# Keeping ten of twelve narrowed weight slices on chip in a recurrent attention and feed-forward kernel

## The chip, the cores and the metric

The kernel runs on one core of a Trainium2 chip. The core has a matrix engine (TensorE, PE in the profile, with its weight loads as PEld), a vector engine (VectorE, DVE), a scalar engine (ScalarE, ACT), GpSimd (POOL) and a sync engine (SyncE, SP) that does nothing here but issue transfers. Data lie in DRAM or in on-chip memory of 128 partitions; matmul results go to a small accumulator memory (PSUM). Transfers (DMA) are issued by SP, and by POOL for the attention's inputs, and are moved by 16 DMA engines. The metric is the time of one execution in device microseconds; less is better.

## The reference

Two blocks follow each other. The first is a recurrence over 768 tokens with a 40 x 40 state for each of 4 x 8 sequences; the second is a gated feed-forward layer on all 3072 tokens.

```python
for t in range(S):                     # batch 4, heads 8, S 768, head_dim 40
    y[:, :, t] = einsum('bhd,bhde->bhe', rt, state)
    Sa = einsum('bhde,bhe->bhd', state, at)
    state_decay = state * wt[:, :, None, :] - einsum('bhd,bhe->bhde', Sa, bt)
    state = state_decay + einsum('bhd,bhe->bhde', vt, kt)
x = y.transpose(0, 2, 1, 3).reshape(3072, 320)
xn = x / sqrt(mean(x * x) + 1e-06) * rms_g
g, val = xn @ w_gate, xn @ w_val       # 320 x 1536 each
out = (silu(g) * val) @ w_out          # 1536 x 320
```

The inputs of the attention are float32. The three weight matrices come as float64 and have to be narrowed to float32 by the kernel's own arithmetic.

## The kernel before

**Attention.** The tokens are cut into 24 chunks of 32, and all 32 sequences are worked on at once. `front(c)` (line 712) loads a chunk, turns it with matmuls against a unit matrix and builds, level by level (spans of 1, 2, 4, 8, 16 tokens), the products of keys and decays; its triangular matrices go through DRAM (tile `sB`) to be laid out one per partition. `inverse(c)` (line 821; the first four chunks use `early_inverse`, line 839) inverts them on VectorE in some 60 small steps with a multiply tile `tmp`, and sends them back through DRAM (`sY`). `main(c)` (line 871) does the part that depends on the chunk before: from state `ST` a right-hand side `Xs`, from it the values `VU`, the new state, a turned copy `vut` of the values, the scores, their masked levels `As`, and the read-out into `y` by level. `y` is then turned, normalised into `x`, turned again and written to the feed's input tile `xg`.

**Feed-forward.** `feed(g)` (line 1001) takes two chunks, 256 tokens, once both are there. It goes through the 12 slices of the weights in pairs, up in even groups and down in odd ones: `h64` and `h` matmuls of the gate and the value half, a Silu on ACT into `sg`, a product on VectorE into `hT`, and `out` matmuls that add into the accumulator `po`. After the last pair ACT copies `po` to tile `o`, and four transfers write it out. A slice is a tile `wf` of 128 x 960 float32 (480 KB); there are six such tiles (`WB = 6`). A narrowed slice lives in DRAM (`sW`), and a feed loads what its six tiles don't hold from the feed before: all 12 slices in the first group, 10 in the second, 6 in each of the ten others, 82 in all.

**Narrowing.** `narrow(f, part)` (line 1037) turns one half of a slice from float64 to float32. It loads the raw words into a `wf` tile that serves as staging, has ACT make the scale from the exponent in three operations into a scratch tile (`ex`, `o` or the second `xg`, in turn), has VectorE join the mantissa in three operations, and stores the half to `sW`. This is done 24 times, during the first 200 us or so.

**Order.** A recording layer (`Plan`, line 270) takes every operation as a piece with an engine and what it depends on. `plan.issue(ORDER, PAIRS)` then hands the pieces to the engines in the sequence that the text `ORDER` (line 33) gives, number by number, relative to the first piece not yet issued; `PAIRS` (line 253) names the accumulator pair that each group of matmuls takes. A dash in `ORDER` issues one filler matmul of the unit matrix into an unused part of `po` (line 1077). So each engine's sequence, SP's and POOL's queues of transfers among them, is fixed by that text; engines wait for each other by semaphores only. Buffers of a kind are handed out in turn by `Turns` (line 561). Since nearly every operation is recorded by a helper, the profile shows helper lines: 545 matmuls, 548 turns by matmul, 503 VectorE, 523, 526 and 529 ACT, 532, 535 and 538 POOL, 542 transfers.

Of the kernel before, what the change touches and what calls it, by code (L numbers as in the profile page):

```python
# [7 lines left out]
FP32 = mybir.dt.float32  # L8
# [9 lines left out]
P = 128  # L18
C = 32
LEVELS = (1, 2, 4, 8, 16)  # L20
CG = 2
WB = 6
# [11 lines left out]
- - 4 - 327 - 328 - - - 6 453 5 7 8 9 10 - 11 12 13 14 15 - 16 17 19 18 20 25 26 21 316 325 - - 313 314 324  # L34
323 - 326 318 - 315 317 93 74 83 3 94 85 73 84 82 - 320 46 43 50 61 38 - - - 60 - - 445 444 455 49 58 44 27 56
62 - 333 41 36 48 54 70 - 441 66 53 59 45 638 29 - 32 28 456 55 451 - - - 442 - 334 339 - - 337 335 338 340
349 350 23 - 342 343 354 24 353 22 355 348 351 352 - 344 - 362 336 366 364 95 - 345 367 346 - - - 347 379 360
- - - 361 363 - 359 365 - 375 75 76 376 78 - 79 - 387 77 356 357 - - 373 - 86 378 371 377 - 80 452 446 454 443
57 - 525 636 37 458 34 368 461 - 374 372 89 386 - 369 383 358 462 - 384 370 466 464 465 385 463 478 98 483 495
- 380 467 381 87 468 395 477 - - 470 471 482 - - 481 472 96 492 382 88 494 97 - 99 - 491 476 493 0 328 123 - -  # L40
102 0 - 100 320 - - 121 112 390 389 387 388 102 - - 111 123 392 471 477 487 - 478 486 - 472 98 - - 488 391 79
103 485 473 88 - - - 89 505 626 61 631 69 598 524 633 621 31 67 66 37 395 632 - - 482 - 62 623 622 28 635 625
- 33 396 624 29 397 398 399 483 400 - - 498 401 402 403 404 405 406 407 - - - - - - - 494 499 484 504 - - 394
500 511 502 496 - 104 - 408 409 410 501 411 412 413 414 - 386 - 415 - 503 416 417 418 419 420 421 422 - 641
105 646 - 106 645 643 - 642 - 107 - 423 - 424 425 - 108 497 - 510 - 644 495 426 328 99 330 329 577 427 - - 506
508 509 109 317 319 120 - 90 - 124 647 521 513 - 125 648 113 114 - 115 657 - 522 131 132 576 - 339 507 127 650
651 656 128 - 428 110 142 517 516 - 652 143 518 515 429 - 653 658 512 660 661 - 116 - 654 - 659 117 655 567
860 70 38 - 45 457 65 63 445 446 448 870 861 871 458 447 430 50 - 662 126 568 669 - 133 134 135 578 581 580
579 672 674 - 664 - - - 118 - - - 519 - 520 - - - 431 - - 432 434 433 - 435 - 436 670 437 438 569 572 570 573
571 129 663 673 675 136 137 138 525 683 - 526 527 671 684 467 528 665 529 667 679 668 682 530 531 532 687 680  # L50
686 533 534 535 536 537 538 539 540 685 541 676 677 542 514 543 544 545 546 547 548 549 550 551 552 553 554 -
119 151 140 162 160 - 163 802 141 999 152 666 582 - 574 144 678 681 583 688 147 148 689 555 1000 172 0 761 90
131 535 653 105 516 546 - - 551 - 555 - 564 - 99 659 121 657 658 660 549 550 553 554 552 654 113 650 106 - 114
109 547 655 548 115 116 117 589 590 600 118 0 406 656 590 600 508 548 554 547 825 579 657 700 701 816 509 131
101 643 115 550 551 552 118 642 119 647 702 703 116 117 124 1083 125 126 652 134 653 511 110 512 143 513 510
553 556 557 558 658 559 560 - 120 561 654 831 514 132 826 835 834 515 832 133 135 833 127 128 129 659 660 661
662 663 664 665 666 667 138 142 - 121 516 517 136 137 836 704 706 655 144 708 705 707 - 139 840 - 668 669 670
671 841 - 852 672 848 140 851 853 673 147 674 - 675 148 - 676 865 677 863 861 0 683 - 689 700 694 685 690 684
459 868 693 707 581 708 717 732 734 582 15 579 716 548 712 580 549 713 550 714 719 715 432 585 23 - - 33 21 0
- 394 11 33 32 13 0 26 25 16 861 683 - 417 418 862 681 419 851 749 750 671 571 0 708 701 569 0 569 - 5 6 416  # L60
531 572 689 532 8 533 534 9 708 535 386 704 566 14 15 16 17 - - 0 - 570 569 568 699 529 530 698 567 0 528 700
0 562 713 711 14 698 715 15 559 7 8 712 560 567 710 406 855 16 - 724 427 854 844 21 417 22 568 569 570 571 575
709 716 667 708 - 528 574 573 - 0 23 22 33 520 - 696 782 563 698 784 785 783 697 705 711 567 568 708 709 569
570 571 - 710 398 399 400 401 713 - 847 836 841 830 840 832 842 831 572 769 - - 839 - 829 521 21 0 16 - - 516
712 24 515 710 709 517 711 514 - 841 843 844 842 565 704 840 6 566 848 0 0 0 760 846 856 853 857 564 565 566
712 567 - 569 570 568 - 759 761 842 713 573 - 515 575 574 843 4 852 14 15 16 703 6 844 7 851 17 847 516 5 0
509 568 1243 703 702 846 850 858 0 9 509 858 14 15 16 860 568 569 570 753 523 21 24 23 1241 22 707 708 846 10
709 839 840 710 859 856 754 755 756 757 841 861 711 712 713 850 853 854 714 715 869 716 - 717 718 866 871 872
852 - 855 0 560 561 32 755 513 756 - 857 840 851 854 852 708 862 709 710 711 712 713 714 853 856 - 759 863 864
# [1040 lines left out]
```

## Time and profile before

| | |
|---|---|
| median of 3 runs | 1030.82 us (1029.99 to 1036.54) |
| profiled execution | 1040.74 us, span 1038.9 us |
| busy: PE, PEld | 991.8 us (95%), 813.4 us |
| busy: DVE, ACT, POOL | 834.2 us, 452.8 us, 310.1 us |
| mean granted TensorE clock | 0.970 |
| DMA | 113.03 MB in 163538 packets |
| loads of narrowed slices | 82 of 480 KB, median 4.7 us to landing |

A group row of the page names line, engine, operation, the tile written and the tiles read, the shape and the count; behind the first bar stand the group's busy time in us and the mean of one in ns, behind the second the engine's idle time just before it and what ended most of that. A row of the windows view gives a stretch, then for each engine its busy time and (x) its instructions, then the granted clock, the mean busy share of the 16 DMA engines and GB/s. A row of the waits reads: who waited, for whom, total us, times, longest. "issue" means that an engine waited for nothing that the profile shows. An engine name with a q is its sequencer, which issues transfers.

### The profile page before, as it was taken

The numbers are of one execution on the slowest core, as the hardware profiler recorded it, in microseconds if no ns is written. First come the engines' busy times: TensorE is split into PE (matmuls) and PEld (weight loads), VectorE is DVE, ScalarE is ACT, GpSimd is POOL, SyncE is SP. The second block draws the span as 40 slices with busy tenths as digits, with TensorE's granted clock in tenths as the row PEclk, the third lists the DMA queues.
The fourth block names the chain that finished last, engine by engine and source line by source line (L and its number), as shares of the span: only waits on it lengthen the run. The fifth ranks groups of instructions, "written<-read, shape, count | busy, mean of one in ns | idle before, by whom it ended". The sixth has DMA issues, their size and how long they took to land.

```text
span 1038.9 us, 56159 instructions
## 1 busy us (share of the span) xinstructions
PE 991.8 (95%) x24900; PEld 813.4 (78%) x24900; DVE 834.2 (80%) x2789; ACT 452.8 (44%) x1019; POOL 310.1 (30%) x554
## 2 busy tenths in 40 slices
PE   8968798999999999999999999999999999999998
PEld 7867686888887888888778877878777788787876
DVE  8878777887979898899888798888899789889310
ACT  5755783644452543433533443352334334341210
POOL 9624422231451224142134232242331331210000
PEclk9886898999999999999999999999999999999999
DMA  7676567465443434534433644343524533422322
GB/s 156 155 171 162 156 130 187 127 160 135 124 87 93 120 73 94 131 72 92 127 71 81 139 79 126 94 84 83 140 61 93 136 67 83 130 44 63 87 65 75
DMA packets 163538, 113.03 MB, mean 109 GB/s; under 512 B 124512, under 2 KB 142880, under 8 KB 163296
## 3 DMA queue, kind: packets, MB, share of 16 engines
q1 hardware_dynamic: 144928, 86.48, 32.9%
q0 software_dynamic: 16192, 22.64, 10.9%
q8 instruction: 195, 3.19, 1.3%
q10 hardware_dynamic: 2176, 0.33, 0.3%
q14 instruction: 47, 0.39, 0.1%
HBM read 93.39 MB, written 15.99 MB: 105 GB/s over the span
## 4 chain that ended last, share of the span: by engine, by line
PE 77%; DVE 10%; DMA 4%; issue 4%; ACT 3%; POOL 1%; SPq 1%; ACTq 0%; DVEq 0%; POOLq 0%
PE ps L545 51%; PE po L545 13%; PE ps L548 7%; PE po L1077 5%; DVE LT L503 2%; DVE tmp L503 2%; DVE Yi L503 2%; DVE K L503 1%; DMA kbn<-in_k_dram 1%; SPq L542 1%; DMA wf<-sW 1%; ACT K L526 1%; DVE As L503 1%; ACT KN L526 1%; DMA kbn<-in_b_dram 1%
## 5 line engine op out<-in xcount | busy, mean ns | idle before, releaser
L545 PE MATMUL ps<-xg,wf 128*128 128x256 f32 (+1 forms) x1728 | 356.8, 394 | 1.6 <-DVE ST L503 0.5
L545 PEld LDWEIGHTS ps<-xg,wf 128*128 128x128 f32 (+1 forms) x1728 | 264.7, 191 | 51.1 <-issue 14.0
L545 PE MATMUL po<-wf,hT 128*128 128x320 f32 x576 | 173.6, 440 | 1.7 <-issue 1.1
L523 ACT ACTIVATE sg<-ps 128x512 f32<-128x512 f32 x72 | 43.1, 598 | 231.5 <-PE ps L545 231.4
L503 DVE TENSOR_TENSOR tmp<-Yi,M 128x60 f32<-128x60 f32 (+24 forms) x620 | 131.4, 212 | 15.2 <-DMA M<-sB 1.2
L503 DVE TENSOR_TENSOR Yi<-Yi,tmp 128x60 f32<-128x60 f32 (+24 forms) x620 | 130.8, 211 | 15.0
L545 PEld LDWEIGHTS po<-wf,hT 128*128 128x128 f32 x576 | 103.9, 190 | 37.8 <-issue 2.0
L1077 PE MATMUL po<-ident 128*128 128x128 f32 x580 | 104.0, 315 | 5.9 <-POOL wan L538 3.3
L526 ACT COPY KN<-ps 128x640 f32<-128x640 f32 x96 | 66.5, 693 | 87.4 <-DVE LT L503 57.9
L542 POOL DMA_DIRECT2D kbn<-in_b_dram x92 | 53.6, 585 | 169.7 <-PE ps L545 168.2
L503 DVE TENSOR_TENSOR K<-K,T 128x512 f32<-128x512 f32 (+1 forms) x192 | 93.1, 491 | 4.7 <-ACT K L526 3.2
L1077 PEld LDWEIGHTS po<-ident 128*128 128x128 f32 x580 | 83.1, 210 | 15.5 <-POOL wan L538 3.3
L503 DVE TENSOR_TENSOR hT<-ps,sg 128x512 f32<-128x512 f32 x72 | 49.4, 687 | 53.0 <-ACT sg L523 52.7
L503 DVE TENSOR_TENSOR As<-ps,msi 128x256 f32<-128x256 f32 (+1 forms) x186 | 82.9, 477 | 8.7 <-PE ps L545 7.4
L545 PE MATMUL ps<-Ab,K 40*60 40x56 f32 (+2 forms) x4608 | 78.3, 217 | 11.3 <-issue 6.8
L545 PEld LDWEIGHTS ps<-Ab,K 40*60 40x60 f32 (+2 forms) x4608 | 68.6, 129 | 22.9 <-issue 12.9
L542 POOL DMA_DIRECT2D VU<-in_v_dram x92 | 53.9, 588 | 108.0 <-PE ps L545 57.0
L526 ACT COPY K<-K 128x256 f32<-128x256 f32 (+1 forms) x168 | 73.1, 446 | 29.6 <-DVE K L503 15.1
L542 POOL DMA_DIRECT2D wn<-in_w_dram x92 | 52.2, 569 | 104.7 <-DVE KN L503 81.6
L542 POOL DMA_DIRECT2D kbn<-in_k_dram x92 | 53.7, 586 | 86.0 <-PE ps L545 83.4
L545 PE MATMUL ps<-As,KN 128*40 128x32 f32 x3072 | 71.5, 204 | 8.0 <-issue 8.0
L545 PEld LDWEIGHTS ps<-As,KN 128*40 128x40 f32 x3072 | 64.8, 123 | 16.9 <-issue 13.3
(137 smaller groups left out, 1469.9 us busy)
## 6 DMA issues: line engine op xcount, KB each, us to landing
wf<-sW SPq DMA_DIRECT2D x82, 480.0 KB, 4.7
M<-sB SPq DMA_DIRECT2D x80, 128.0 KB, 3.4
rn<-in_r_dram SPq DMA_DIRECT2D x24, 160.0 KB, 3.9
out_dram<-o SPq DMA_DIRECT2D x48, 80.0 KB, 3.1
kbn<-in_k_dram POOLq DMA_DIRECT2D x92, 40.0 KB, 3.5
kbn<-in_b_dram POOLq DMA_DIRECT2D x92, 40.0 KB, 3.3
wan<-in_w_dram POOLq DMA_DIRECT2D x46, 80.0 KB, 3.0
wan<-in_a_dram POOLq DMA_DIRECT2D x46, 80.0 KB, 3.2
```

Of the source, the lines that this page charges most:

```text
L503: plan.add("DVE", kind, lambda at: fn(at(o), *m(at)), [o], aps(*args))
L523: plan.add("ACT", "act", lambda at: nc.scalar.activation(at(o), at(a), f, **kw), [o] + aps(acc), [a])
L526: plan.add("ACT", "copy", lambda at: nc.scalar.copy(at(o), at(a)), [o], [a])
L542: plan.add(by, "dma", lambda at: queue.dma_start(out=o, in_=i), [o], [i])
L545: return o, lhsT, rhs, lambda at: nc.tensor.matmul(at(o), lhsT, rhs, start=start, stop=stop, skip_group_check=True)
L548: return o, i, ident, lambda at: nc.tensor.transpose(at(o), i, ident)
L1077: plan.warm = lambda: nc.tensor.matmul(po_[:, 0, DM:DM + P], ident, ident, start=False, stop=False, skip_group_check=True)
```

## The change

The count of `wf` tiles goes from 6 to 10. The first eight slices are narrowed straight into the tiles where the feeds read them; slices 8 to 11 still go through DRAM, and slices 0 and 1 are stored there as well, once each as a whole, because slices 10 and 11 take their tiles in turn. The first feed loads the last four slices, each further one two: 4 + 11 x 2 = 26 loads. Staging uses four of the tiles for the first twelve halves and two for the last twelve; the scratch of the narrowing has two tiles in place of three.

Room for the four added tiles comes from tiles that share: `vut` and `Xs` lie inside `As` (`vut` in the place of levels 1 and 2, `Xs` in that of level 16), two of the mask's five levels lie in `vut` during the set-up, the state's two halves overlap their padding, `tmp` and `y` have one buffer in place of two, the last key tile (`KN` of 32) two in place of three, `sg` and `hT` become one tile with three buffers, and the feed's output is copied into the feed's own `xg` tile. `ORDER` and `PAIRS` are new texts: the dashes go from 290 to 301, SP's pieces from 634 to 564, the TensorE groups stay 905.

```diff
-WB = 6
+WB, DIRECT = 10, 8
...
-    vut_ = Turns(1, [P, 2, N, 64], "vut")
-    msk = const.tile([P, len(LEVELS), C], FP32, name="msk")
+    As_ = Turns(1, [P, len(LEVELS), NI, 2, 16], "As")
+    spare = As_.tiles[0].rearrange("p j n i t -> p (j n i t)")
+    vut_ = spare[:, 0:2 * N * 64].rearrange("p (u n t) -> p u n t", u=2, n=N)
+    Xs_ = spare[:, 4 * NI * 32:4 * NI * 32 + 8 * D].rearrange("p (u e) -> p u e", u=2)
+    msk = const.tile([P, len(LEVELS) - 2, C], FP32, name="msk")
...
-    ST_ = Turns(2, [P, N, 2, 64], "ST", whole)
+    TOP = 64 + D
+    ST_ = Turns(2, [P, N, TOP], "ST", whole)
...
-    KN_ = {l: Turns(3, [P, NI * D], f"KN{l}_") for l in LEVELS[1:] + (32,)}
+    KN_ = {l: Turns(2 if l == 32 else 3, [P, NI * D], f"KN{l}_") for l in LEVELS[1:] + (32,)}
...
-    tmp_ = Turns(2, [P, 80], "tmp")
+    tmp_ = Turns(1, [P, 80], "tmp")
...
-    y_ = Turns(2, [P, NI, C], "y", whole)
+    y_ = Turns(1, [P, NI, C], "y", whole)
...
-    sg_ = Turns(2, [P, 2 * GT], "sg")
-    hT_ = Turns(2, [P, 2 * GT], "hT")
-    o_ = Turns(1, [P, CG, DM], "o")
-    ex_ = Turns(1, [P, WH], "ex", dtype=I32)
-    ex_.tiles += [t.rearrange("p q d -> p (q d)").bitcast(I32) for t in (o_.tiles[0], xg_.tiles[1])]
+    sg_ = Turns(3, [P, 2 * GT], "sg")
+    ex_ = Turns(0, [P, WH], "ex")
+    ex_.tiles += [sg_.tiles[2].bitcast(I32), xg_.tiles[1].rearrange("p q d -> p (q d)").bitcast(I32)]
...
-            hh, sg, hT = plan.room(), sg_.next(), hT_.next()
+            hh, hT = plan.room(), sg_.next()
...
-                if nth >= WB or g == 0 or g == 1 and nth > 0:
+                if nth >= (DIRECT if g == 0 else WB):
                     dma(wf, sW[f + e])
...
-            act(sg, hh[:, 0], AF.Silu)
-            tt(hT, hh[:, 1], sg, MUL)
+            act(hT, hh[:, 0], AF.Silu)
+            tt(hT, hh[:, 1], hT, MUL)
...
-        o = o_.next()
+        o = x.rearrange("p k t -> p (k t)")[:, 0:CG * DM].rearrange("p (q d) -> p q d", q=CG)
         copy(o, po[:, :, 0:DM])
...
-    def wf_at(g, f):
+    def wf_at(f):
-        return wf_.tiles[f % 2 if g == 0 else (FT - 2 - f // 2 * 2) % WB + f % 2]
+        return wf_.tiles[(FT - 2 - f // 2 * 2) % WB + f % 2]
...
-        rw = wf_.tiles[k if k < 2 else 2 + (k - 2) % 4].bitcast(I32).rearrange("p (f w) -> p f w", w=2)
+        rw = wf_.tiles[2 + (k % 4 if f < DIRECT - 2 else k % 2)].bitcast(I32).rearrange("p (f w) -> p f w", w=2)
...
-        stt(exf, low, 2.0 ** 20, exf, ADD, MUL)
-        dma(sW[f][:, part * WH:(part + 1) * WH], exf)
+        to = slice(part * WH, (part + 1) * WH)
+        stt(wf_at(f)[:, to] if f < DIRECT else exf, low, 2.0 ** 20, exf, ADD, MUL)
+        if f >= DIRECT:
+            dma(sW[f][:, to], exf)
+        elif f < 2 and part:
+            dma(sW[f], wf_at(f))
```

The new `ORDER` and `PAIRS` are left out here. The changed places of `main` that only rename tiles (`vut`, `Xs`, the views of `ST`) are left out too.

More of the change, by code (lines that the diff above doesn't have):

```diff
@@ L592 @@
     eye = const.tile([P, C // 4, C], FP32, name="eye")
[L593 removed]
+    row, column, bits, same = (vut_[:, 0, k, 0:C].bitcast(I32) for k in range(4))
     same = same.bitcast(FP32)
+    mask = lambda j, p=slice(0, P): msk[p, j - 2:j - 1] if j > 1 else vut_[p, 0, 4 + j:5 + j, 0:C]
     for t, pattern, each in ((row, [[0, C]], 1), (column, [[1, C]], 0)):
@@ L611 @@
         for i in range(2):
-            pcopy(msi[half(i), j, i:i + 1].rearrange("p n (g l) -> p n g l", l=l), side(msk[half(i)], l, 1)[:, j:j + 1])
+            pcopy(msi[half(i), j, i:i + 1].rearrange("p n (g l) -> p n g l", l=l), side(mask(j, half(i)), l, 1))
     blank(eye, 0.0)
@@ L686, with two @@
     Z = {}
-    TOP = 64 + D
+    def two(t):
+        one = t[:, 0:1, 0:1]
+        return bass.AP(one.tensor, one.offset, [list(one.ap)[0], [TOP, N], [64, 2], [1, D]])
     def turned(t, at, outs=TOP, by=half, w=64):
```

297 lines of the change are left out of this document (145 added, 152 removed), and 165 rows, old and new, of the table ORDER.

## The prediction

> **What bounds the kernel now.** The page comes first: busy shares, the granted clock in 40 slices, DMA.
>
> ```profile
> span 1038.9 us, 56159 instructions
> PE 991.8 (95%) x24900; PEld 813.4 (78%) x24900; DVE 834.2 (80%) x2789; ACT 452.8 (44%) x1019; POOL 310.1 (30%) x554
> ...
> PEclk9886898999999999999999999999999999999999
> DMA  7676567465443434534433644343524533422322
> ...
> L1077 PE MATMUL po<-ident 128*128 128x128 f32 x580 | 104.0, 315 | 5.9 <-POOL wan L538 3.3
> ```
>
> TensorE is busy 95% of the span, so its stream, issued in a fixed order, is the clock of the kernel. It holds three things. The real work is 991.8 - 104.0 = 887.8 us. The filler matmuls of line 1077, one for each dash of the written order (290 dashes, two records each), take 104.0 us, or 104.0 / 290 = 0.36 us a dash. Idle is 1038.9 - 991.8 = 47.1 us. Two answers of the windows view, of all engines and then of line 1077 alone, show where the second and third lie: the first 200 us, and the rest.
>
> ```profile
> 0.00:200.00 200.00, 171.86 (x4572) 149.88 (x4572) 157.79 (x467) 129.41 (x278) 87.26 (x176) 0.86 0.66 155
> 200.00:960.00 760.00, 745.44 (x19434) 606.65 (x19433) 659.87 (x2288) 310.91 (x718) 221.70 (x376) 1.00 0.42 100
> 960.00:1039.00 79.00, 74.53 (x901) 56.87 (x899) 16.51 (x36) 12.53 (x25) 1.11 (x2) 1.00 0.25 75
> ...
> 0.00:200.00 200.00, 63.84 (x380) 54.41 (x380) 0.86 0.66 155
> ```
>
> The first numbers after a stretch are the busy times of PE, PEld, DVE, ACT and POOL; the last three are the granted clock, the DMA share and GB/s. Of 47.1 us idle, 28.1 lie before 200 us, with a clock of 0.86 and the DMA engines at 0.66. What ends PE's idle time is in the view of waits, first for the 200 us, then for the rest:
>
> ```profile
> PE ps L545 <- issue: 17.1, 11, 4.2
> ...
> PE ps L548 <- DMA wan<-in_a_dram: 1.0, 1, 1.0
> ...
> PE ps L548 <- DMA kbn<-in_k_dram: 0.9, 1, 0.9
> PE po L1077 <- issue: 0.7, 1, 0.7
> ...
> PE ps L545 <- issue: 7.8, 10, 2.0
> ...
> PE po L545 <- issue: 1.1, 1, 1.1
> ```
>
> PE hardly waits for another engine. It waits for "issue": nothing in the profile holds it, it just has no instruction, 17.8 us early and 8.9 us late. Two of the late stalls stand in the chain; windows round them and SP's timeline just before them show the company they keep:
>
> ```profile
> 739.43 1.96 issue
> ...
> 818.42 1.84 issue
> ```
>
> ```profile
> 734.00:740.00 6.00, 5.43 (x153) 4.09 (x152) 5.59 (x24) 3.42 (x7) 0.21 (x1) 1.00 0.97 318
> 742.00:746.00 4.00, 4.00 (x11) 3.23 (x12) 3.99 (x10) 1.41 (x3) 0.09 (x1) 0.57 0.07 12
> 812.00:818.00 6.00, 6.00 (x135) 4.67 (x133) 5.37 (x24) 2.61 (x7) 4.62 (x9) 1.00 0.97 240
> 821.00:824.00 3.00, 3.00 (x28) 2.60 (x26) 0.78 (x5) 1.75 (x4) 1.25 (x3) 0.50 0.24 61
> ...
> 731.25 1.82 SPq L542 DMA_DIRECT2D wf<-sW  x2
> ...
> 734.80 1.40 SPq L542 DMA_DIRECT2D wf<-sW  x2
> ...
> 812.49 0.89 SPq L542 DMA_DIRECT2D wf<-sW  x2
> ```
>
> Both stalls follow six microseconds in which the DMA engines were 0.97 busy, against 0.42 in that part, and the burst holds weight loads from DRAM, 480 KB each. After each the clock falls to about half for some 3.4 us. The page's DMA queues have one of kind instruction:
>
> ```profile
> q8 instruction: 195, 3.19, 1.3%
> ```
>
> 195 packets of 16.4 KB pass through the same 16 engines as the data. My reading: a burst of weight transfers delays the next block of PE's instructions; PE runs dry; the clock drops.
>
> [...]
>
> **The change part by part.**
>
> *Traffic.* The loads of weight slices from DRAM fall from 82 to 4 + 11 x 2 = 26, and the stores of narrowed halves from 24 of 240 KB to 8 of 240 KB and 2 of 480 KB.
>
> ```profile
> DMA packets 163538, 113.03 MB, mean 109 GB/s; under 512 B 124512, under 2 KB 142880, under 8 KB 163296
> ...
> wf<-sW SPq DMA_DIRECT2D x82, 480.0 KB, 4.7
> ```
>
> That is 56 x 0.4915 = 27.5 MB and 2.95 MB less of 113.03. In the late part 101 x 0.76 + 6 = 82 MB pass now; at least 74 - 26 = 48 loads go, 23.6 MB or 29%, and with them the largest single transfers. The first 200 us hold these:
>
> ```profile
> DMA packets 49343, 30.99 MB, mean 155 GB/s; under 512 B 32672, under 2 KB 46496, under 8 KB 49296
> ...
> wf<-sW SPq DMA_DIRECT2D x8, 480.0 KB, 5.4
> ...
> sW<-ex SPq DMA_DIRECT2D x7, 240.0 KB, 3.0
> ```
>
> With its two sister groups (three scratch tiles take turns), 21 stores or 5.2 MB lie there, of which at most 2.95 remain; the eight loads, 3.9 MB, go or come later, since the four loads of the first feed need tiles that staging holds to its end. That is 6.1 of 31 MB, 20%. The raw weights stay.
>
> *Late gain.* Cost of the late stalls now: 8.9 us, and for the slow clock 4 x 0.43 + 3 x 0.50 = 3.2 us, 12.1 in all. The two stalls above with their clock are 1.96 + 1.84 + 3.2 = 7.0; I take them as gone. Of the other 5.1 I take 29%, 1.5. Together -8.5; bounds 0 and -12.1.
>
> [...]
>
> *Early gain.* Stalls 17.8 us; clock 200 x 0.14 = 28 us, of which PE was busy 0.86: 24 us. Together 41.8. By traffic a fifth would go, 8.4; by the late part's share (8.5 of 12.1) 29. I take 30%, 12.5, nearer the first, because the raw loads remain. Bounds 0 and -21: beyond that VectorE would do its 157.8 us in under 179, more than the 659.87 of 760 (87%) it shows later.
>
> *Filler.* The new order has 301 dashes, 290 before: 11 x 0.36 = +3.9 us, eight of them before the second feed. They run whether PE needs them or not.
>
> *The shared room.* TensorE's groups stand in nearly the same sequence in both orders; real work is equal in kind and count (905 groups). New waits: the negated right-hand side of a chunk now lies in the score tile's last level, so its ACT write waits for the last chunk's level-16 read-out; the turned value copy waits for all five level groups of the chunk before; y has one buffer; the last key tile two. Behind these writes on ACT stand the chunk's own evacuations, and PE would wait for them. But counted in PE groups of the new order, from the second chunk on at least 10 lie between the level-16 read-out and the right-hand side that waits for it, at least 13 between the last level and the turned copy, and 14 or more between y's last read and its next write, but for two chunks with 5 and 2. A group is 32 or 16 matmuls of 0.2 us, several us for ten. And PE's late waits on other engines are small now; the two longest groups:
>
> ```profile
> PE po L1077 <- ACT o L526: 1.9, 2, 1.0
> ...
> PE ps L545 <- DVE LT L503: 0.7, 2, 0.5
> ```
>
> I take 0; the bound above is that these double, with some smaller ones +5. Hidden by the feed's matmuls between; if that cover went, each chunk would show one copy of about a microsecond.
>
> *Queues.* SP issues 70 transfers fewer. Loads that waited there for PE's output matmuls held up the mask and inverse transfers behind them; PE waited for DMA for 1.0 + 0.9 us in all, so 0. The output now leaves from the feed's own input tile; its transfers must land before the feed two further on has that tile filled, with 45 pieces of the order between in the closest case. The smaller scratch (one multiply tile) is VectorE's alone, which runs in order: 0.
>
> *Sum.* -8.5 - 12.5 + 3.9 = -17.1 us. Against the profiled execution's own 1040.74 us (its span 1038.9 and 1.8 round it): 1023.6, a ratio of 0.9836. The runs' median is 1030.82; times 0.9836 that is **1014 us**.
>
> **The rivals.**
>
> *Stalls that don't care.* PE drains blocks faster than they come in dense stretches of small matmuls, whatever the data queues do; or the stalls just move to other bursts (the mask transfers, GpSimd's loads). For it: in the chain the longest early stall
>
> ```profile
> 66.36 4.20 issue
> ```
>
> stands amid raw weight loads that stay. Against it: the two 0.97 windows. Then the gains vanish, +3.9 is left: 1044.6 x 0.9905 = 1035 us, within 1%. [...]
>
> *Slower: narrowing through two buffers.* The last twelve halves have two staging tiles in place of four, and two exponent buffers in place of three throughout.
>
> ```profile
> L523 ACT ACTIVATE o<-wf,ctop x8: 720/742/766, 21.1 to 185.4; 128x480 f32<-128x480 int16 x8
> ...
> L503 DVE SCALAR_TENSOR_TENSOR o<-wf,o x8: 640/656/659, 34.7 to 199.3; 128x480 f32<-128x480 f32 x8
> ...
> wf<-in_moe_w_gate_dram SPq DMA_DIRECT2D x12, 256.0 KB, 4.2
> ...
> 110.81 0.65 DVE L503 SCALAR_TENSOR_TENSOR ex<-wf,ex 128x480 f32<-128x480 f32 x1
> ...
> L503 DVE SCALAR_TENSOR_TENSOR ex<-wf,ex x8: 635/652/659, 22.5 to 207.3; 128x480 f32<-128x480 f32 x8
> ```
>
> Half 22 stayed from ACT's start at 185.4 to VectorE's end at 199.3 + 0.66, 14.5 us, and 4.2 for its load: 18.7. Two buffers then give a half each 9.4 us, 113 us for twelve, against about 90 in which the halves from 110.81 to 207.3 came now: +23 us on the first feed, which stands in PE's stream ahead of all the rest. It decides once a half stays longer than about 15 us. Against it: with three ACT operations as long as the first shown (0.74) and three of VectorE as the last (0.66), the bare work of a half is 4.2 + 2.2 + 2.0 = 8.4 us, and the new order takes its ACT and VectorE steps closer together. With the late gain and the filler: 23 + 3.9 - 8.5 = +18.4, that is 1059.1 x 0.9905 = 1049 us.
>
> That the loads stay after all is excluded: the issue order has 26.
>
> **How the numbers follow.** The forecast has 0.59, the first rival 0.23, the second 0.18. A measurement of this kernel tells about 1% from no change: 1020.5 and 1041.1. Of the forecast's spread (both gains near their lower bounds give within 1%) I put 0.50 faster and 0.09 the same; the first rival is 0.22 the same and 0.01 slower, the second 0.18 slower. So 0.50, 0.31, 0.19. Range: both gains at their ends, -12.1 - 21 + 3.9 = -29.2, is 1002; no gain with +5 of new waits is 1040. That leaves the second rival out.
>
> **What would show it.** Right: 26 weight loads; late issue stalls under 4 us and no slow clock behind 200 us; early clock above 0.86, early stalls under 17.8 us; filler 108 us; PE waits on ACT and VectorE as small as now. Wrong: issue stalls as large as now with a smaller DMA share (first rival); the first feed ending well behind the present one, with PE waiting for VectorE's weight tiles (second); or PE waits on score, y or key tiles in every chunk.

## The result and the profile after

The changed kernel takes 1041.13 us (median of 20 runs, 1033.80 to 1047.23) against 1033.90 us of the kernel before (median of 20 runs on the same chip, 1027.66 to 1044.80). The ratio is 1.0068, 95% interval [1.0041, 1.0094]: it is slower by 0.7%, where 1.6% faster was forecast. That lies within the 1% that a measurement was said to tell from no change, just above the range's end of 1040. Where runs of a kernel lie more than 1.5% above its fastest one, a ratio leaves them out, so that here and below it can differ from the quotient of the medians beside it.

The executions of either kernel spread over 13 to 17 us, and the two profiled ones happen to stand in the reverse order of the medians: that of after took 1037.9 us (span 1035.8), that of before 1040.74. So two single traces can't be subtracted here. Each reading below is held against further traces of the same kernels.

The page of the changed kernel, the lines that answer to those shown of before: busy time, clock and DMA in 40 slices, packets, filler, weight loads.

```profile
span 1035.8 us, 56030 instructions
PE 991.2 (96%) x24922; PEld 819.2 (79%) x24922; DVE 834.2 (81%) x2789; ACT 451.4 (44%) x1019; POOL 309.5 (30%) x553
...
PEclk9976799999999999999999999999999999999999
DMA  8555447444233334233153243254224332420110
...
DMA packets 153457, 82.54 MB, mean 80 GB/s; under 512 B 123392, under 2 KB 139712, under 8 KB 153216
...
L1080 PE MATMUL po<-ident 128*128 128x128 f32 x602 | 104.7, 312 | 5.1 <-DVE po L572 3.3
...
wf<-sW SPq DMA_DIRECT2D x26, 480.0 KB, 5.0
```

The traffic is gone as announced: 26 loads for 82, 82.5 MB for 113.0. TensorE's own time is the same, 991.2 us for 991.8, 104.7 of it filler. The windows view of after, in the columns explained for before:

```profile
0.00:200.00 200.00, 177.21 (x4719) 156.21 (x4723) 163.83 (x490) 130.21 (x280) 86.41 (x173) 0.89 0.58 127
200.00:960.00 760.00, 744.64 (x19469) 607.93 (x19457) 652.95 (x2264) 308.77 (x715) 222.02 (x378) 1.00 0.34 71
960.00:1036.00 76.00, 69.38 (x752) 55.11 (x752) 17.42 (x35) 12.40 (x25) 1.09 (x2) 1.00 0.13 37
```

From 200 to 960 us a fifth of the DMA engines' busy time has gone (share 0.34 for 0.42) and 29% of the bytes per second (71 GB/s for 100), and PE is busy for as long as before. The waits of PE in after, first those before 200 us, then those after (line; what was waited for; us in total, times, longest):

```profile
PE ps L540 <- issue: 5.2, 6, 1.7
PE ps L540 <- DVE LT L498: 3.6, 3, 1.6
PE po L1080 <- DVE po L572: 3.3, 1, 3.3
PE ps L540 <- ACT aP L521: 1.6, 1, 1.6
PE ps L540 <- POOL msi L530: 1.3, 1, 1.3
...
PE po L1080 <- issue: 0.5, 1, 0.5
...
PE ps L540 <- issue: 8.9, 9, 2.8
PE ps L543 <- issue: 1.4, 2, 0.9
PE ps L540 <- DVE A L498: 1.4, 1, 1.4
...
PE ps L540 <- DMA LT<-sY: 1.0, 4, 0.3
```

Before 200 us the issue stalls are 6.1 us (with one more row of 0.4) where they were 17.8; but the waits for other engines and DMA have grown from 10.2 to 16.3 us, the sums of all such rows of the view. The three longest of them in before, beside those already shown there:

```profile
PE po L1077 <- POOL wan L538: 3.3, 1, 3.3
PE ps L545 <- DVE K L503: 1.4, 1, 1.4
PE ps L545 <- DVE Ab L503: 1.3, 1, 1.3
```

Behind 200 us the issue stalls are 10.3 us, not fewer than the 8.9 of before. The longest of them stands in the chain of after (start, us, what):

```profile
807.49 2.84 issue
```

The windows of all engines before and after it:

```profile
801.00:807.00 6.00, 6.00 (x161) 4.76 (x159) 5.45 (x22) 1.85 (x5) 5.28 (x10) 1.00 0.95 168
810.40:813.80 3.40, 3.40 (x37) 2.77 (x38) 1.37 (x6) 0.73 (x2) 0.00 (x0) 0.50 0.22 44
```

And from the timelines of GpSimd and SP, the first and last of eleven transfers that GpSimd issues there, and the weight load:

```profile
800.31 0.58 POOL L537 DMA_DIRECT2D kbn<-in_b_dram  x1 [7.53 <-PE ps L540]
...
806.76 0.65 POOL L537 DMA_DIRECT2D wan<-in_w_dram  x1 [0.72 <-PE ps L543]
...
800.07 1.92 SPq L537 DMA_DIRECT2D wf<-sW  x1
```

It is the picture of 739 and 818 us again: six microseconds with the DMA engines 0.95 busy, a stall, half the clock for 3.4 us. Only now the burst consists of one weight load and of a chunk's inputs, mostly transfers of 40 KB that GpSimd issues, and of the mask transfers. The change doesn't touch those.

The chain of work that ended last has changed as well; the page gives the shares of the span that lie on each engine, first before, then after:

```profile
PE 77%; DVE 10%; DMA 4%; issue 4%; ACT 3%; POOL 1%; SPq 1%; ACTq 0%; DVEq 0%; POOLq 0%
```

```profile
PE 58%; DVE 22%; DMA 8%; SPq 4%; issue 4%; ACT 2%; DVEq 0%; POOL 0%; ACTq 0%; POOLq 0%
```

DVE's share says little, since it goes from 10 to 21% between three traces of the kernel before. Transfers and SP's queue together have 3 to 5% in those three, and 9 to 13% in the five traces of the new order that are compared below. One row of the waits goes with it: PE waits for the inverses that come back through DRAM (`LT<-sY`), 1.0 us here. Behind 240 us that wait comes in all eight traces of the changed kernel with its own late order (0.6 to 3.7 us) and in none of the eight of the kernel before with its own. It is small, but the change brought it.

### The profile page after: what moved, and what is told of

Same layout as the page of the kernel before. It is cut to its first block, busy times and chain, and to the rows that moved or that the text cites. A ratio compares the mean times of both kernels' runs of the same rounds, so it can differ in the third digit from the quotient of the medians.

```text
span 1035.8 us, 56030 instructions
## 1 busy us (share of the span) xinstructions
PE 991.2 (96%) x24922; PEld 819.2 (79%) x24922; DVE 834.2 (81%) x2789; ACT 451.4 (44%) x1019; POOL 309.5 (30%) x553
## 2 busy tenths in 40 slices
DMA packets 153457, 82.54 MB, mean 80 GB/s; under 512 B 123392, under 2 KB 139712, under 8 KB 153216
## 4 chain that ended last, share of the span: by engine, by line
PE 58%; DVE 22%; DMA 8%; SPq 4%; issue 4%; ACT 2%; DVEq 0%; POOL 0%; ACTq 0%; POOLq 0%
PE ps L540 38%; PE po L540 10%; PE ps L543 5%; PE po L1080 5%; SPq L537 4%; DMA M<-sB 4%; DVE tmp L498 4%; DVE Yi L498 3%; DVE LT L498 3%; DVE K L498 2%; DVE As L498 2%; DMA sB<-LT 2%; DVE y L498 1%; DVE sg L498 1%; DVE wf L498 1%
## 5 line engine op out<-in xcount | busy, mean ns | idle before, releaser
L540 PEld LDWEIGHTS ps<-xg,wf 128*128 128x128 f32 (+1 forms) x1728 | 263.3, 190 | 46.4 <-issue 10.3
L540 PE MATMUL po<-wf,sg 128*128 128x320 f32 x576 | 174.4, 441 | 0.0
L540 PEld LDWEIGHTS po<-wf,sg 128*128 128x128 f32 x576 | 104.8, 191 | 36.1 <-issue 1.1
L1080 PE MATMUL po<-ident 128*128 128x128 f32 x602 | 104.7, 312 | 5.1 <-DVE po L572 3.3
L1080 PEld LDWEIGHTS po<-ident 128*128 128x128 f32 x602 | 87.4, 211 | 16.4 <-issue 6.9
L498 DVE TENSOR_TENSOR sg<-ps,sg 128x512 f32<-128x512 f32 x72 | 49.4, 687 | 44.9 <-ACT sg L518 44.6
```

The source lines that it names most:

```text
L498: plan.add("DVE", kind, lambda at: fn(at(o), *m(at)), [o], aps(*args))
L540: return o, lhsT, rhs, lambda at: nc.tensor.matmul(at(o), lhsT, rhs, start=start, stop=stop, skip_group_check=True)
L1080: plan.warm = lambda: nc.tensor.matmul(po_[:, 0, DM:DM + P], ident, ident, start=False, stop=False, skip_group_check=True)
```

## The experiments

All ratios are to the kernel before on the same chip. "Late part" means from the end of the first feed (ACT's copy of `po`) to that of the last one.

### The two kernels once more

The changed kernel as it is, and the kernel before as it is, twice for one more trace each.

> The changed kernel once more, for a second trace beside the ones below. Measured so far: 1.007 of the kernel before, interval 1.004 to 1.009. Expected again 1.003 to 1.011. Open from the first pair of traces: the stalls named issue fell from 17.8 to 6.1 us in the first 200 us but not later (8.9 to 10.3 us), and the profiled run of before was 7 us above its own median. If the stalls of one execution are chance, this trace will show another late sum than 10.3, somewhere between 2 and 15 us.

Measured: 1039.93 us, 1.009 [1.0055, 1.0126]. The slowdown holds, though its size is uncertain: the medians of all runs, this one and 1033.59 us of the kernel before, give 1.0061.

> The kernel before once more, for a second trace of it: its first trace (1040.74 us) lies above the median of its own runs (1033.9). Theory D, the stalls named issue and the slow clock are chance that differs from one execution to the next: late stalls between 2 and 12 us and other places than 739 and 818 us; the time follows their sum. If they are fixed by the transfers, the stalls stand at the same places again.

> A third trace of the kernel before, as the one above: chance says other places and another sum, a fixed cause says stalls at 739 and 818 us of the first trace again.

Measured: 1029.45 and 1035.42 us. The late issue stalls are 8.0 and 8.7 us, as in the first trace (8.9). Of the two stalls that the prediction took apart, the chain of the first repeat has the one before the matmul of `A` and `K`, and that of the second has both:

```profile
731.73 1.42 issue
```

```profile
737.41 2.04 issue
814.90 1.56 issue
```

So the first of the two came at its place in all three traces and the second in two of them; but neither repeat shows a slow clock behind 200 us (their mean clocks of 0.982 and 0.971 are accounted for by 0.91 and 0.85 in the first 200 us), though one stall is as long as the 1.96 us that was followed by half the clock: the 235 matmuls behind 1.96 us took 9.70 us, behind 2.04 us 8.01. In the five traces of the changed kernel's unaltered order the stall at 807 to 815 us came each time (2.0 to 3.1 us). In the first of them half the clock followed for 3.4 us, in the second the clock was 0.58 from 811 to 814 us, and in the one with an output tile of its own (further below) the page gives 8 tenths for the slice from 809 to 836 us.

The ends of the first feed show that the early part didn't get shorter: before 235.5, 225.9 and 232.7 us, after 230.4 and 231.7. The late part is 798.3, 796.6 and 795.8 us before, 800.4 and 798.9 after.

Some of the runs below leave the early part of an order as it is, which gives eight traces of each:

| first 200 us | old order, eight traces | new order, eight traces |
|---|---|---|
| PE's stalls of "issue" | 10.6 to 17.8 us | 2.9 to 9.5 us |
| PE's waits for engines and DMA | 9.3 to 14.1 us | 16.3 to 23.0 us |
| granted clock | 0.85 to 0.91 | 0.88 to 0.91 |
| end of the first feed | 225.9 to 235.5 us, mean 231.0 | 227.2 to 235.3 us, mean 231.6 |

The stalls do go and the other waits do come in their place. The 17.8 us that the prediction counted is the highest of its eight, and the clock of the two orders can't be told apart.

### What the late traffic costs

Four, then all six of the weight loads of each feed from the third on are cut to 8 KB in the kernel before. The matmuls then take whatever weights the tile held, so the output isn't the layer's; the operations on the engines stay the same.

```diff
-                    dma(wf, sW[f + e])
+                    w_ = 16 if g > 1 and nth < 10 else WF     # second run: g > 1 alone
+                    dma(wf[:, 0:w_], sW[f + e][:, 0:w_])
```

> The kernel before, in its own order, with 40 of its 82 weight loads (four of six in each group from the third on) cut from 480 KB to 8 KB, so that the matmuls of those slices use what the tile held before; nothing else changes. The prediction's reading, transfers cause the late stalls: those stalls fall under 4 us and the time to 0.988 to 0.995. Its first rival, the stalls do not care: 0.998 to 1.002 with late stalls of 5 to 12 us.

> The kernel before with all six loads of each group from the third on (60 of 82) cut from 480 to 8 KB, so that these groups use the weights that lie in the tiles. 29 MB less, against 20 in the run with four thin loads. Theory T: 0.990 to 0.996. Theory N: 0.998 to 1.002.

Measured: 1027.25 us, 0.9969 [0.9933, 1.0006], and 1023.61 us, 0.9895 [0.986, 0.993]. The other way round, the changed kernel with four copies of 480 KB from DRAM to DRAM added to each feed from the third on:

```diff
+            if g > 1 and nth in (4, 6):
...
+                    for e in range(2):
+                        nc.sync.dma_start(out=sX[(n + e) % 8][:, 0:WF], in_=sW[8 + fs[e] % 4])
```

> The changed kernel with the late traffic of the kernel before put back: in each group from the third on four more transfers of 480 KB, from DRAM to DRAM, issued by SP between the feed's pairs; nothing waits for them. Theory T, late traffic costs some 5 us (the thin loads gave 0.997, interval 0.993 to 1.001): 1.009 to 1.016 of the kernel before. Theory N, traffic costs nothing: 1.004 to 1.010. In both, late stalls named issue near 9 us if they come from TensorE's own consumption of instructions.

Measured: 1046.27 us, 1.0122 [1.0082, 1.0162]. The packet rows of the pages, first with all six loads cut, then with the added copies:

```profile
DMA packets 163538, 84.03 MB, mean 82 GB/s; under 512 B 132192, under 2 KB 150560, under 8 KB 163296
```

```profile
DMA packets 159217, 102.21 MB, mean 98 GB/s; under 512 B 124032, under 2 KB 140352, under 8 KB 158976
```

The late waits of PE, first with four loads cut, then with six:

```profile
PE ps L545 <- issue: 9.6, 10, 2.9
```

```profile
PE ps L545 <- issue: 3.7, 5, 1.3
```

The longest late stall in the chain of the run with four loads cut:

```profile
739.27 2.89 issue
```

So the traffic does cost something, and its price is of the size that the prediction gave: 29.0 MB less are worth 1.05% or 10.9 us. The 19.7 MB more in the changed kernel cost 0.3 to 0.5% by the two ratios of that kernel, with overlapping intervals. Whether the price goes with the amount can't be told: 19.3 MB less give 3.2 us by the ratio and 6.3 us by the medians of all runs (1027.25 and 1033.59). The stalls don't go with it. With two of six loads left the stall at 818 us is gone, but the one at 739 us stands as before, longer even, and the late stalls are 9.6 us (that trace is the slowest of twelve executions, 1037.94 us); with none left both have gone and 3.7 us remain, in one trace. Two loads for each feed is what the changed kernel keeps. The changed kernel moves less than the thinned one (82.54 MB for 84.03) and is yet 1.0068 / 0.9895 = 1.0175 times as slow. Something worth 1 to 2% works against the gain, and it isn't the amount of traffic.

### The shared tiles

`vut`, `Xs`, `y` and the last key tile get their own room again in the changed kernel, with the order unchanged; the room comes from weight slices 3 and 5, which use the tiles of 2 and 4, so that here too the output isn't the layer's.

```diff
-    vut_ = spare[:, 0:2 * N * 64].rearrange("p (u n t) -> p u n t", u=2, n=N)
-    Xs_ = spare[:, 4 * NI * 32:4 * NI * 32 + 8 * D].rearrange("p (u e) -> p u e", u=2)
+    vut_ = const.tile([P, 2, N, 64], FP32, name="vut")
+    Xs_ = const.tile([P, 2, 4 * D], FP32, name="Xs")
...
+    y_.tiles.append(const.tile([P, NI, C], FP32, name="y1"))
...
-        return wf_.tiles[(FT - 2 - f // 2 * 2) % WB + f % 2]
+        return wf_.tiles[(FT - 2 - f // 2 * 2) % WB + (0 if f in (3, 5) else f % 2)]
```

> The changed kernel in its own order, with the turned value copy and the right-hand side in tiles of their own, two y buffers and three last key tiles; room for them comes from two weight tiles fewer (slices 3 and 5 are narrowed over slices 2 and 4 and stand for both). Theory B, the shared room makes the changed kernel slower: 0.998 to 1.003 of the kernel before. Theory A, the order does (it was written for the sharing, and holds the same distances without it): 1.004 to 1.010, the same as the changed kernel.

Then the output tile alone gets its own room:

```diff
+    o_ = Turns(1, [P, CG, DM], "o")
...
-        o = x.rearrange("p k t -> p (k t)")[:, 0:CG * DM].rearrange("p (q d) -> p q d", q=CG)
+        o = o_.next()
```

> The changed kernel with an output tile of its own instead of the room of the normed input, and nothing else changed, the order of issue neither. The same computation. If the shared output room costs something in the new order, the ratio to the kernel before falls from 1.007-1.009 to 1.000-1.004; if the order was made so that it costs nothing, it stays at 1.005-1.010.

Measured: 1039.61 us, 1.0045 [1.0012, 1.0077], and 1040.14 us, 1.0066 [1.0035, 1.0096]. The intervals overlap those of the changed kernel (1.0068 and 1.009). By the ratios the sharing costs some 2 to 5 us in its own order, not clear of noise, and the output's room nothing that can be told. Most of the 1 to 2% isn't there.

### The other kernel's order

Each kernel in the order of the other: the pieces that both have are issued in the other's sequence, a piece that isn't ready is put back until it is, and extra loads follow where they can. Only `ORDER` and `PAIRS` change.

> The kernel before, with its six weight tiles and all its own tiles, in the issue order of the changed kernel (its 70 additional transfers put in as soon as what they need has been issued; 115 pieces, nearly all of feeds and narrowing, had to move back a little). Theory A, the new order with its 11 more fillers costs the time and the traffic gives nothing: 1.004 to 1.012. Theory B, the shared tiles and the two staging buffers cost it: 0.995 to 1.002. Theory C, the new order costs and the smaller traffic gives something back: above 1.012.

> The changed kernel with all its tiles, in the issue order and with the 290 fillers of the kernel before (70 transfers fall out, 80 pieces had to move back, most of the narrowing). Theory A, the order costs: 0.995 to 1.003. Theory B, the shared tiles cost: 1.005 to 1.02. Theory C, the order costs and the traffic gives: 0.98 to 0.995.

Measured: 1187.07 us, 1.1527 [1.1475, 1.1579], and 1093.80 us, 1.0626 [1.0577, 1.0676]. The first is no clean test: 115 pieces move back, and PE waits 28.4 us for weight loads. The second says more. The first feed ends at 269.7 us, 34 to 44 later than in the traces of before, most likely because the narrowing through two staging tiles doesn't follow the old order. That would be the second rival's mechanism, which the new order avoids; but 80 pieces moved back too, and no run separates the two. And late in the run PE waits for the input tile `xg`; VectorE, which fills that tile, waits 6.2 us for the output's transfers that still read it, and so holds PE up:

```profile
PE ps L545 <- DVE xg L500: 12.0, 3, 4.8
```

Two hybrids separate these: the changed kernel in its own order up to the start of the second feed, and in that of before from there, with an output tile of its own (three pieces move back) and without (19).

> The changed kernel with an output tile of its own (2.5 KB a partition, as before), its own order of issue up to the start of feed 1, and from there the order of the kernel before (without the weight loads that are gone; three pieces move back, 303 dashes). The same computation. If what takes back the gain is the new late order, the late part (end of feed 0 to end of feed 11) falls from about 800 us to 790-796 and the ratio to the kernel before is 0.990-0.997. If it is the shared small tiles (y, Xs, vut, KN32), or an early part that is no shorter than before's, the late part stays at 798-803 and the ratio at 1.004-1.010. If the old order doesn't suit the shared tiles, as in the run with the old order throughout, waits of PE on DVE of over 8 us come up and the ratio is above 1.01.

> As the hybrid with the old late order, but with the output tile in the room of the normed input, as the changed kernel has it (19 pieces move back). The same computation. If the old order and the shared output room get in each other's way, as the 12.0 us of waits of turns on xg in the run with the old order throughout say, the late part is 8-15 us longer than in the hybrid with an output tile of its own, and the ratio is 0.01 above that one's; if those waits came from that run's narrowing, the two agree within 0.004.

Measured: 1050.73 us, 1.0171 [1.0125, 1.0218], and 1073.55 us, 1.0401 [1.0362, 1.0439]. The view of waits of the second from 235 us on:

```profile
PE ps L545 <- DVE xg L500: 12.8, 3, 4.8
PE ps L545 <- issue: 7.7, 5, 2.9
PE ps L542 <- issue: 4.9, 6, 1.4
```

The shared output room costs 2.3% with the old late order (and the 16 more pieces that move back) and nothing that can be told in the new one. And the old late order doesn't win the gain back, as I had thought by then, even where no tile stands in its way: the first hybrid is slower than the changed kernel. In it PE waits for other engines for only 4 us behind 235 us, yet its late part is 814.8 us for 800, with 15.8 us of issue stalls and a clock of 0.99 from 230 to 1030 us (1.00 in the changed kernel).

### Filler taken out

The dashes behind the start of the second feed are taken out of the order, 90 of 290 before and 88 of 301 after; a line of `ORDER` of before:

```diff
-365 548 - 551 - 552 553 391 - 392 - 393 394 395 - 526
+365 548 551 552 553 391 392 393 394 395 526
```

> The kernel before without the 90 fillers that its order has behind the start of the second feed (90 x 0.36 = 32 us of TensorE). If TensorE's stream alone sets the time there, the time falls by up to 32 us, 0.97. If the fillers stand where TensorE would wait anyway (for VectorE above all), 0.995 to 1.005, with the waits of PE on DVE and ACT grown by some 25 to 30 us, and perhaps more slow clock.

> The changed kernel without its 88 fillers behind the start of the second feed (32 us). As for the kernel before: 0.975 to 0.98 of the kernel before if TensorE's stream sets the time, 1.00 to 1.01 if other engines do. If its 11 more fillers are what makes it slower than the kernel before, the two kernels without late fillers should still differ by the early eight, 3 us or 0.3%, not by 0.8%.

Measured: 1052.91 us, 1.0196 [1.0164, 1.0228], and 1049.08 us, 1.0161 [1.0122, 1.02]. The late waits of PE, before without late filler, then after without it:

```profile
PE ps L544 <- issue: 19.0, 22, 3.7
PE ps L547 <- issue: 2.8, 4, 1.2
```

```profile
PE ps L538 <- issue: 19.2, 20, 4.1
PE ps L541 <- issue: 4.5, 4, 2.1
```

In the first 38 us of filler are gone (its row has 65.7 us, for 104.0) and the kernel is 20 us slower. Issue stalls rise from 8.9 to 21.8 and from 10.3 to 23.7 us, and from 200 to 960 us the granted clock is 0.98 and 0.99, where it was 1.00. The page of the first has more:

```profile
PE 979.3 (94%) x24720; PEld 793.8 (76%) x24720; DVE 834.1 (80%) x2789; ACT 451.9 (43%) x1019; POOL 308.8 (29%) x554
```

Without filler PE was busy for 979.3 - 65.7 = 913.6 us, where it was 887.8: the same matmuls take 26 us longer, 27 and 34 against the two repeats. Part of that is the clock: behind 200 us it loses some 13 us by estimate (0.032 of the 1047.1 us of the span, less 0.10 of the first 200 us), where the two slow stretches of 3.4 us at 0.50 in the first trace of before lose 3.4.

Without late filler the changed kernel isn't the slower one any more: 1.0161 against 1.0196, with overlapping intervals. The expectation, which put its slowness on the 11 additional dashes, had the difference stay. This points to how filler and order fit, and not to the count of dashes.

In another run half the early filler of the changed kernel is taken out (106 of the 213 dashes ahead of the second feed):

> The changed kernel without every second of the 213 fillers ahead of the second feed: 106 x 0.36 = 38 us of TensorE's early stream. If that stream sets the early time, as the prediction's sum has it, 0.965 to 0.975 of the kernel before. If VectorE, ACT and the transfers set it, the early part ends where it did or later, with PE's waits on them up by some 35 us and more slow clock: 1.005 to 1.02.

Measured: 1080.98 us, the median of six runs from 1063.24 to 1086.08; the ratio, 1.0349 [1.0271, 1.0428], rests on the two fastest. Even the fastest run is 22 us slower than the median of the changed kernel. The trace is that of the slowest run; the late waits of PE in it:

```profile
PE ps L538 <- issue: 24.9, 20, 2.3
PE ps L541 <- issue: 5.4, 6, 1.6
```

The expectation looked for the loss in the early part, and most of it isn't there. The first feed ends at 237.6 us, against 227.2 to 235.3 in the eight traces above, while the late part takes 840.2 us instead of 800, with 30.3 us of issue stalls and a clock of 0.97 from 200 to 960 us, where it was 1.00. Yet behind the start of the second feed the order is that of the changed kernel, dash for dash. In this trace, then, the late stalls depend on what was issued long before them too, and not only on the filler and the transfers beside them. What carries that over, no run shows.

### Filler added, and filler moved

In the new order only one dash lies between 746 and 867 us of its first trace, and stalls stand there in each trace. 17 dashes are put between 700 and 975 us in the changed kernel, 18 into the stretches without any in the kernel before.

```diff
-426 429 726 558 559 749 560 561
+426 429 726 - 558 559 749 560 561
```

> The changed kernel with 17 dashes more (318 for 301), put into the stretches between 700 and 975 us that have almost none: up to now two dashes lie between 746 and 867 us, and the stalls of issue at about 725, 794, 807-815, 890-902 and 979 us stand there in every trace of this order. They cost 17 x 0.35 = 6 us of filler. If filler lets the fetch of PE's instructions catch up, the late issue stalls fall from 9-10 us to 3-5, the slow stretch at 811-814 us goes, and the ratio to the kernel before is 1.002-1.006, below the changed kernel's 1.007-1.009. If the filler only adds its own time there, as the prediction's term said, the stalls stay and the ratio is 1.010-1.016.

> The kernel before with 18 dashes more (308 for 290) in its stretches without any (468-538 us, 773-945 us and before the stalls at 700 and 733-741 us). They cost 18 x 0.36 = 6.5 us of filler. If filler lets the fetch catch up, the late issue stalls fall from 8-9 us to 3-5 and the ratio is 0.997-1.002; if it only adds its own time, 1.005-1.008.

Measured: 1040.22 us, 1.0056 [1.0023, 1.009], and 1048.07 us, 1.0126 [1.0087, 1.0166]. The late waits of the first, then of the second:

```profile
PE ps L540 <- issue: 3.3, 7, 0.8
...
PE ps L543 <- issue: 1.0, 2, 0.7
```

```profile
PE ps L545 <- issue: 8.5, 8, 2.8
PE po L1077 <- issue: 2.6, 1, 2.6
```

In the changed kernel the filler takes the stalls away (4.3 us for 10.3, the 807 us one among them) and pays for itself, no more: the time is that of the changed kernel within noise. In the kernel before it doesn't take them away, and the loss of 13 us is twice its own 6.5. Place decides. So the last run changes the place alone: the 90 late dashes of the kernel before, each 8 to 24 places earlier or later, with the pieces in their old sequence.

```diff
-365 548 - 551 - 552 553 391 - 392 - 393 394 395 - 526
+365 548 - - - 551 552 553 391 392 393 394 395 526
```

> The kernel before with its 90 dashes behind the start of feed 1 each moved by 8 to 24 places in the order, earlier or later at random; the pieces keep their order, and the number of dashes is 290 as before. The same computation, the same work on every engine. If the places of the filler against the stream of instructions carry some per cent of the time, the late issue stalls rise above 12 us and the ratio is 1.007-1.02: then any new order has to win that back first, and the changed kernel's 0.7-0.9 per cent is of the size of such a loss. If only the amount of filler matters, the ratio is 0.998-1.003.

Measured: 1047.93 us, 1.0118 [1.0065, 1.0171]. Its page and the first late waits:

```profile
span 1048.5 us, 56159 instructions
PE 1002.6 (96%) x24900; PEld 819.0 (78%) x24900; DVE 834.2 (80%) x2789; ACT 451.4 (43%) x1019; POOL 309.6 (30%) x554
...
L1077 PE MATMUL po<-ident 128*128 128x128 f32 x580 | 105.1, 317 | 5.3 <-POOL wan L538 3.3
```

```profile
PE ps L545 <- issue: 8.3, 11, 1.8
...
PE po L545 <- issue: 1.6, 2, 0.9
```

The same work, instruction for instruction, and 1.2% more time (by the interval 0.65 to 1.7%): the expectation's ratio, though not by its means. The late issue stalls are 9.9 us, not above 12. The clock over the span is 0.970, where the three traces of before have 0.970, 0.982 and 0.971. Most of the difference sits in PE's own time, which takes in the slow clock: 1002.6 - 105.1 = 897.5 us without the filler, against 887.8, 879.7 and 886.2 in the three traces of the kernel before. The changed kernel, at 1.0068, isn't slower than this rearranged kernel before; the intervals overlap.

## Why the prediction was wrong

Two steps of the sum failed, the gain of 12.5 us from the early stalls and the gain of 8.5 us from the late ones, and one thing was put at nothing without a measurement, the new order.

**Early gain, -12.5.** The stalls went as the term said and further (17.8 to 6.1 us); but the first feed ends where it did. What failed is the assumption that a stall that goes is time that goes. Nothing was said there of what is late next: without those stalls PE waits for VectorE, ACT and transfers instead, 16.3 us for 10.2, and eight more dashes run by the end of the first feed. "PE hardly waits for another engine" had passed over these 10.2 us. That the engines had caught up while PE stood is the plain reading of it. The run with half the early filler fits, since TensorE work taken out there didn't end the first feed sooner (237.6 us); its clock was lower too (0.74), so it is no proof. The base was high as well: seven more traces of the old early order have 10.6 to 13.5 us of stalls, not 17.8, and a clock of up to 0.91. Over eight traces of each order the gain is 0, the bound that the sum gave it.

**Late gain, -8.5.** The size of what traffic is worth was near: -3.2 and -10.9 us in the two runs with thinned loads. The step that failed is "I take them as gone", of the two stalls. That weight loads have a part in them is borne out, since both go when all of these loads are thinned. But two loads for each feed remain, and they can be enough: the stall at 739 us stood with two loads left, and in the new order one weight load among a chunk's inputs precedes 2.84 us at 807. The rule of 29% less traffic, 29% less of the other stalls, has no support either: they stay at 10.3 us at 71 GB/s. The slow clock, 3.2 us of the term, isn't a fixed companion of these two stalls: both repeats of the kernel before had stalls there (1.42 us; 2.04 and 1.56 us) and no slow clock. The first rival had named what happened ("the stalls just move to other bursts (the mask transfers, GpSimd's loads)"), and its 1035 us within 1% is the case nearest to the result.

That these stalls are waits for PE's instructions is inferred from their company, and no view shows it. What the runs show is that less late filler brings 13 us more of them (21.8 us for 8.9 in the kernel before, 23.7 for 10.3 in the changed one).

**Filler, +3.9.** The kind of the term was wrong. "They run whether PE needs them or not" holds, but taking 90 out cost 20 us net, 17 more in one set of places cost nothing, and 18 more in another cost twice their duration. Here no price per dash holds; what counts is where the dashes stand. Of the additional dashes 13, not eight, stand ahead of the second feed's start (213 for 200); by the end of the first feed eight more have run. The filler's row didn't show the 3.9 us either: 104.7 and 101.3 us in two traces of after, 103.3 to 106.7 in three of before.

**Shared room and queues, 0.** Right within the bound of +5: some 2 to 5 us for the tiles by the ratios, not clear of noise, none to be told for the output. For the queues 0 was nearly right: the new wait for the inverses' transfers is 0.6 to 3.7 us behind 240 us. The cover named, the matmuls between, is a property of the new order: with the old one the output's room alone costs 2.3%.

**Second rival, 1049.** Its mechanism is the likely reason why the first feed ends 34 to 44 us later with the old order. The new order keeps clear of it: its first feed ends where that of before does.

**What the sum left out.** It took the order as neutral: TensorE's groups stand in nearly the same sequence, so only the count of dashes entered. But a mere shift of 90 dashes costs the kernel before 1.2%, 18 dashes more cost it 1.3%, and the hybrid's mixed order 1.7%. A new order can draw anew from effects of that size: stalls of issue, slow clock, and PE's time in its matmuls. At about the late traffic of before the changed kernel is 1.2% slower (with the added copies), and less traffic gives a part of that back; what remains is 0.7%. That the new order is what costs this is the reading that is left, with at most a few us for the tiles; the two kernels without late filler, between which no loss is left, agree with it. No run shows it by itself, since neither kernel can be run in the other's order unharmed. What makes the same matmuls take 10 to 34 us longer when filler moves or goes is open as well, beyond the part that the slow clock has in it: the profile's matmul ends are modelled, so that short waits may be booked there as busy time.

## What to carry to other kernels

Before a stall's time is counted as a gain, ask for each stretch which engine is ready next if the stall goes; and look at a second trace before two single stalls carry a term. In a kernel that is bound by one engine's stream and has been laid out instruction by instruction, a new order can have a cost of its own as large as the gain sought (here 90 moved dashes cost 1.2%, where 1.6% was forecast): measure it with a placebo (the same work with only the filler moved) and hold the forecast against that. In this kernel filler between dense stretches isn't priced by its own duration.

## What the hardware showed that was not expected

- Filler that only adds matmuls can shorten the run: 38 us of it removed made the kernel 20 us slower, with 21.8 us of late issue stalls for 8.9.
- Filler removed ahead of the second feed lengthened what comes behind it, in an unchanged order: 840.2 us of late part for 800, in the slowest of six runs.
- The same instructions with 90 filler pairs moved by 8 to 24 places take 1.2% longer.
- The clock fell to half (0.50) for 3.4 us after stalls of 1.84, 1.96 and 2.84 us: from 820.7 to 824.1 and from 742.2 to 745.6 us before, from 810.4 to 813.8 us after. A stall of 2.04 us in a repeat of the kernel before brought none (235 matmuls in 8.01 us behind it, against 9.70 behind the 1.96 us), nor did one of 2.89 us with four loads cut (231 in 7.94 us), so the length of the stall alone doesn't decide.
- 40 copies of 480 KB more (19.7 MB) cost the changed kernel 0.3 to 0.5%, not clear of noise, while the share of the DMA engines in the late part rose only from 0.34 to 0.39.
